# Query projection moved into the first FFN's Strassen units, w2 sums in PSUM, two products on one bank: a new order for a one-core attention and FFN kernel

## The chip, the cores and the metric

The kernel runs on one core of a Trainium2 chip, in one launch. The metric is the device time in microseconds (us). Besides the time of plain runs there is one profiled execution, whose span (first to last instruction) is a little shorter than the time of its run. The engines have the names of the profile: PE (matrix products) with its weight loads PEld, DVE (vector), ACT (activation), POOL (GpSimd) and SP, which issues the DMAs.

## What is computed

`x` is 2048 tokens by 512 features. Layer norm gives xn, and then

```python
q, k, v = xn @ wqkv                                # 32 heads of 16
phi_q = [softmax(q @ w_phi), softmax(-q @ w_phi)]  # per head, 16 wide each
phi_k = [softmax(k @ w_phi), softmax(-k @ w_phi)]
kv = phi_k.T @ v ; z = sum over tokens of phi_k    # per head, not causal
s = (phi_q @ kv) / (phi_q @ z + 1e-6) @ wo
h = xn @ w1 + b1 ; h = h * tanh(softplus(h))       # Mish, 1792 wide
g = silu(h @ w2)
out = x + s * g
```

All of it is in fp32.

## The kernel before, in words

**Products.** Each fp32 product is three fp32r products: an operand is split into a high part (an ACT copy) and a low part (a subtraction on DVE or POOL). The main unit of work on PE is one 128x128 weight tile against 512 columns, "128x512" in the profile. Layer norm (`norm`, L348) works on 16 tiles of 128 tokens; PE transposes each (`pt`), and its high and low parts stay as `xT`. The head map w_phi is folded into the query and key weights on PE (`folded`, L298: `wqf`, `wkf`).

**Keys and values** use a Strassen scheme of seven products for a pair of tiles (`kv_a` to `kv_d`, L470 to L496; banks `kx`, `ky`, `kz`); pair 0 is done plainly. In `kv_a` bank `kx` is copied out (`held`), bank `kz` gets the second product, and DVE adds the two in SBUF (`plus`). `k_soft` makes the two softmaxes of a tile: for tile t, DVE takes maximum and minimum (`kTm<-kp`), subtracts twice (`kTe`), ACT takes the exponential, DVE sums, inverts and scales. `kv_acc` (L518) then adds phi_k transposed times v to the PSUM bank `kvp`, with many small 32x32 matmuls. `sums` (L867) reads `kvp` once all 16 tiles are in.

**Queries** are projected plainly: `q_proj` (L505) makes 12 matmuls of 128x512 for each of the 16 tiles, copies the bank to SBUF (`qs`) and sends it to DRAM (`qd`). `q_soft` (L510) reads it back in another arrangement (`qp`, four DMAs a tile) and does the same softmax. `den` (L534) multiplies by z (`ez`), sums (`tz`), inverts, scales the features, and transposes them into `ph`. `num` (L554) takes four tiles together: 64 small matmuls `pn`. `att_out` (L571) multiplies by wo (`pw`) and sends the result to DRAM (`so`).

**The first FFN product** uses 14 units: two halves q of the tokens by seven blocks b of 256 features, each of seven products (`ffn1a` to `ffn1d`, L689 to L711; banks `fx`, `fy`, `fz`). The x operands are sums of tiles kept in DRAM (`scr`, `scrT`). `load_g` (L650) loads them for one half in 14 DMAs of 512 KB (names `fb..`, `ft..`). `GROUPS` (L33) says which blocks share a load: there are three loads here, L0 to L2. `ffn1a` has the form of `kv_a`: `held`, `fz`, then `plus` on DVE (`ha<-ha,fz`). `prep1` (L586) makes the sums of a block of w1 (`w1a`, `w1s` with h or l).

**The second FFN product** (`ffn2a` to `ffn2f`, from L739; banks `x`, `y`, `z`) uses sums of w2, which `prep2`, `prep2d`, `prep2a` and `prep2b` (L613 to L634) make in SBUF (`w2r`, `w2c`, `w2s`, `w2t`), with the splits (`w2x`, `w2t`, `w2sb`) on DVE or POOL. `final` (L811) puts silu, product and sum together.

**Order.** `ORDER` (L34) is the order in which parts of the program are built. `SCHED` (L49) is the order in which the single operations are issued; a letter behind a number picks the engine (V, G or A) where two could do it. `PLACE` (L134) gives each tile its buffer. The pools are `slot` (38 big buffers), `s2` (15 of 128x512), `rq` (5), `ps` (the 8 PSUM banks) and a few more. Each engine takes its instructions strictly as listed, and `Program.issue` emits all of them, so each has line L192 in the profile (L194 after the change). Groups are therefore told apart by the tiles' names.

Of the kernel before, what the change touches and what calls it, by code (L numbers as in the profile page):

```python
# [10 lines left out]
F32 = mybir.dt.float32  # L11
# [5 lines left out]
P = 128  # L17
# [10 lines left out]
SLOTS, S2, RQ = 38, 15, 5  # L28
# [4 lines left out]
GROUPS = ((0, 1, 2, 3), (4, 5, 6))  # L33
ORDER = """  # L34
wq1 N0 wk0 N4 wk1 N1 K0 wq0 Ka1 Q4 wv0 wv1 V0 N5 N2 ws0 Q0 Q2 N8 Q5 ws1 N12 N3 V4
Q8 Kb1 Q1 N6 Q12 ws2 Ka3 N7 Ka2 Kc1 N9 ws3 Kb2 N10 Q6 Kd1 Kc2 Q9 N13 N11 Kd2 Kb3 Ka5 Ka4
Kc3 Ka7 K4 Kd3 Ka6 N14 Kb4 Kb6 Kc4 Q11 N15 Kc6 Q14 Kd4 Kb5 Q13 A0 P2 A1 Q10 Q3 Kd6 A2 A3
P1 A4 Kc5 Q7 Kb7 Q15 Kd5 L0 Kc7 Fa2 Kd7 P0 Fa1 S1 Fa0 S0 Fb1 Fc1 Fb2 Fb0 Fd1 Fc2 A5 A6
S2 A7 P3 Fa3 Fb3 Fc3 Fc0 Fd2 b1 S3 Fd3 z D0 D1 Fd0 L1 Fa7 S4 Fa8 Fa9 Fa10 D2 Fb7 S6
D3 Fb8 Fc8 Fb9 Fd8 P4 Fc9 Fb10 Fd9 S10 Fa11 Fc10 Fc7 Fd10 D4 P5 P6 S5 Fd7 Fb11 Fc11 Fa13 D5 Fb13  # L40
Fa12 S7 S8 Fc13 Fb12 Fc12 Fd13 D6 L2 S9 Fd11 Fa4 Fb4 D7 S13 Fd12 wo0 Fa5 Fc4 Fa6 Fb6 Fc6 Fb5 Fd6
Fc5 wo1 U0 D8 D9 Fd4 Fd5 U1 R0 D10 O7 Ga0 O4 R1 O0 S11 Ga1 D11 R2 O3 S12 Ga2 O2 R3
D12 Ga3 D13 S14 R4 O6 Ga4 O1 O5 R5 D14 Ga5 S15 D15 R6 U2 Ga6 U3 T0 O13 Gb0 T1 Gb1 T2
Gb2 O11 T3 Gb3 T4 Gb4 T5 O8 Gb5 T6 Gb6 B0 Gc0 O14 B1 Gc1 B2 Gc2 B3 Gc3 O15 B4 Gc4 B5
Gc5 B6 O9 Gc6 C0 Gd0 C1 Gd1 O12 C2 Gd2 C3 Gd3 C4 O10 Gd4 C5 Gd5 C6 Gd6 E0 Ga7 Ga8 Ga9
E1 Ga10 Ga11 Ga12 E4 Ga13 Gb7 E5 Gb8 Gb9 Gb10 E6 Gb11 Gb12 E7 Gb13 Gc7 Gc8 Gc9 Gc10 Gc11 Gc12 Gc13 E8
E2 E3 E9 E14 E15 E12 E13 Ge7 Ge8 Ge9 Ge10 Ge11 Ge12 Ge13 E10 Gf7 Gf8 Gf9 Gf10 Gf11 Gf12 Gf13 E11
"""
# [156 lines left out]
def block_kernel(ctx: ExitStack, tc: tile.TileContext, x, xt, wqkT, wv, phi, wo, w1, b1, w2, out):  # L205
# [200 lines left out]
    def proj(t, w, name):  # L406
        ps = bank([P, D], f"{name}{t}")
        for i in range(0, KC, 2):
            with one():
                for k in (i, i + 1):  # L410
                    mm3(ps, (xT[t][:, 0, k, :], xT[t][:, 1, k, :]), w[k], k == 0, k == KC - 1)
# [511 lines left out]
```

## Time and profile before

| | |
|---|---|
| plain runs | 491.93, 492.81 and 681.34 us, median 492.81 |
| the profiled execution | 491.45 us, its span 489.7 us |
| PE busy | 477.8 us, 98% of the span |
| DVE busy | 448.3 us, 92% |
| ACT busy | 292.5 us, 60% |
| POOL busy | 267.2 us, 55% |
| DMA | 114.01 MB, mean 233 GB/s |

A group's row in the profile names the engine, the operation, out<-in by the program's names, the shapes and the count; behind the bar stand the busy time, the mean of one in ns, and the idle time just before with the releaser. Matmuls overlap, so the mean of one (some 390 ns) is longer than the distance from one to the next. The same holds of DVE: its records overlap by some 0.08 us, and the distance between starts is what one costs. The profiled execution lies 1.75 us over its span, and the median of the runs 3.1 us over it.

### The profile page before, as it was taken

To read this page: it belongs to the slowest core of one execution; us is meant where nothing else is said; L and a number is where in the kernel's file an instruction comes from. 1 tells how busy PE (TensorE), PEld (TensorE's weight loads), DVE (VectorE), ACT (ScalarE), POOL (GpSimd) and SP (SyncE) were. 2 spreads that over 40 slices of the span, in tenths; PEclk is the share of its full clock that TensorE was granted. 3 is DMA by queue.
4 is the path that set the end of the run, shared out by engine and by line. 5 is a ranking of instruction groups with operands and counts; after the bars stand their busy time and mean duration, and the time that the engine had idled before them with its cause. 6 is when DMAs were issued, how large, how long until landed. Compare 5 with 4: busy or idle time off the path is not lost.

```text
span 489.7 us, 9113 instructions
## 1 busy us (share of the span) xinstructions
PE 477.8 (98%) x3332; PEld 386.9 (79%) x3332; DVE 448.3 (92%) x716; ACT 292.5 (60%) x465; POOL 267.2 (55%) x185
## 2 busy tenths in 40 slices
PE   9999899999999999999999999999899999999995
PEld 9888678888787887888888867868678888888883
DVE  5989999999999999999999989999998977799965
ACT  5998675544262351325434558694795879889531
POOL 2678942323427333164825399968867647541540
PEclk9999999999999999999999999999999999999998
DMA  8524447595979777996999999972247747933276
GB/s 297 200 90 149 193 173 242 183 346 199 331 233 308 264 259 251 301 319 198 349 324 314 322 301 346 338 229 87 104 178 251 229 145 230 299 111 87 86 220 231
DMA packets 71133, 114.01 MB, mean 233 GB/s; under 512 B 6193, under 2 KB 39601, under 8 KB 71089
## 3 DMA queue, kind: packets, MB, share of 16 engines
q1 hardware_dynamic: 70944, 113.18, 68.8%
q8 instruction: 26, 0.43, 0.3%
q10 hardware_dynamic: 144, 0.26, 0.2%
q14 instruction: 19, 0.15, 0.1%
HBM read 71.47 MB, written 41.94 MB: 232 GB/s over the span
## 4 chain that ended last, share of the span: by engine, by line
PE 73%; DVE 10%; issue 3%; DMA 1%; ACT 1%; POOL 0%; DVEq 0%; SPq 0%; ACTq 0%
PE fx L192 16%; PE x L192 14%; PE y L192 8%; PE fy L192 7%; PE kx L192 6%; PE fz L192 4%; PE pw L192 4%; PE q L192 4%; PE ky L192 3%; PE z L192 2%; PE kvp L192 2%; PE kz L192 2%; DVE tz L192 1%; PE pn L192 1%; DMA so<-so 1%
## 5 line engine op out<-in xcount | busy, mean ns | idle before, releaser
L192 PE MATMUL q<-wqh,xT 128*128 128x512 f32 x128 | 42.2, 392 | 0.0
L192 ACT ACTIVATE r<-r,b1t 128x512 f32<-128x512 f32 x56 | 37.7, 713 | 0.1
L192 PEld LDWEIGHTS q<-wqh,xT 128*128 128x128 f32 x128 | 24.0, 188 | 5.2
L192 POOL TENSOR_TENSOR w1sl<-w1s,w1sh 128x1024 fp32r<-128x1024 f32 x7 | 16.8, 2406 | 20.1 <-ACT w1sh L192 16.4
L192 POOL TENSOR_TENSOR rs<-rs,mhalf 128x1 f32<-128x1 f32 x16 | 10.0, 641 | 29.4 <-DVE rs L192 25.1
L192 POOL TENSOR_TENSOR tl<-ts,th 128x1024 fp32r<-128x1024 f32 x8 | 19.4, 2431 | 10.4 <-ACT th L192 5.1
L192 PE MATMUL q<-wql,xT 128*128 128x512 f32 x64 | 25.0, 390 | 0.0
L192 DVE TENSOR_REDUCE tz<-ez 128x64 f32<-128x1024 f32 x16 | 19.3, 1208 | 0.3
L192 ACT ACTIVATE ha<-fx 128x512 f32<-128x512 f32 x14 | 8.2, 594 | 17.6 <-PE fx L192 14.0
L192 ACT ACTIVATE hd<-fx 128x512 f32<-128x512 f32 x13 | 7.7, 595 | 17.7 <-PE fx L192 14.4
L192 ACT ACTIVATE hc<-fx 128x512 f32<-128x512 f32 x13 | 7.6, 594 | 17.7 <-PE fx L192 17.7
L192 POOL TENSOR_TENSOR w1al<-w1a,w1ah 128x768 fp32r<-128x768 f32 x6 | 11.1, 1849 | 12.3 <-DMA scr<-xT 6.5
L192 PE MATMUL kx<-wss,th 128*128 128x512 f32 x56 | 17.6, 394 | 0.0
L192 ACT ACT_TABLE_LOAD x13 | 16.7, 1283 | 1.5 <-PEq L915 1.2
L192 ACT ACTIVATE hb<-fx 128x512 f32<-128x512 f32 x13 | 7.7, 595 | 13.8 <-PE fx L192 12.0
L192 ACT ACTIVATE kp<-kx 128x512 f32<-128x512 f32 x12 | 7.2, 596 | 14.7 <-PE kx L192 10.8
L192 POOL TENSOR_TENSOR mt<-r,r 128x512 f32<-128x512 f32 x7 | 9.5, 1364 | 11.6 <-ACT oh L192 4.4
L192 PE MATMUL pw<-oh,wo0l 128*128 128x512 f32 x32 | 12.6, 392 | 2.2 <-DVE h L192 2.2
L192 POOL TENSOR_TENSOR t<-r,mt 128x512 f32<-128x512 f32 x8 | 12.6, 1573 | 3.2 <-DVE mt L192 1.9
L192 PEld LDWEIGHTS q<-wql,xT 128*128 128x128 f32 x64 | 12.0, 188 | 2.5
L192 POOL TENSOR_TENSOR w2t<-w2t 128x512 f32<-128x512 f32 (+1 forms) x10 | 12.8, 1281 | 0.1
L192 PE MATMUL pw<-oh,wo0h 128*128 128x512 f32 x32 | 12.5, 389 | 0.0
(977 smaller groups left out, 1865.0 us busy)
## 6 DMA issues: line engine op xcount, KB each, us to landing
r<-hd SPq DMA_DIRECT2D x28, 512.0 KB, 5.5
qd<-qs SPq DMA_DIRECT2D x16, 256.0 KB, 4.0
scr<-xT SPq DMA_DIRECT2D x8, 512.0 KB, 6.3
scrT<-th SPq DMA_DIRECT2D x8, 512.0 KB, 4.3
scrT<-tl SPq DMA_DIRECT2D x8, 512.0 KB, 5.9
qp<-qd SPq DMA_DIRECT2D x64, 64.0 KB, 5.2
so<-so SPq DMA_DIRECT2D x16, 256.0 KB, 5.3
sr<-so SPq DMA_DIRECT2D x16, 256.0 KB, 3.6
```

The lines of the kernel that those rows point to most:

```text
L192: getattr(g, m)(*a, **k)
```

## The change

- **Queries.** `proj`, `q_proj` and the way through DRAM go. The folded query weights are written as two more blocks in the form of w1 (`w1a7`, `w1a8`); `prepq` makes their sums; four more units (two halves of the tokens, two blocks) run through `ffn1a` to `ffn1d`. Such a unit's results go by a DVE transpose straight into `qp`.
- **Query softmax.** The sums stay as they are, without an inverse; the product of both sums takes its place in `den`. `rq` has 7 buffers of four values a head.
- **Two products on one bank.** In `ffn1a` and `kv_a`, ACT copies the first product into the bank of the second, PE adds the second to it, and the bank is sent or copied. The DVE sum goes.
- **w2 sums** are formed in PSUM banks, from an ACT copy, with DVE operations that have one operand there; their splits are on DVE alone.
- **Loads.** `GROUPS` has four loads (L0 to L3): blocks 0 to 2, then the two query blocks with block 3, then 4 to 6.
- `final` keeps `u` in SBUF for two token tiles, the head order of wo's rows is another, and `ORDER`, `SCHED` and `PLACE` are new lists.

```diff
-SLOTS, S2, RQ = 38, 15, 5
+SLOTS, S2, RQ = 38, 15, 7
-GROUPS = ((0, 1, 2, 3), (4, 5, 6))
+GROUPS = ((0, 1, 2), (NB, NB + 1, 3), (4, 5, 6))
...
+        if sums is not None:
+            V.tensor_reduce(sums, e, axis=X, op=ALU.add)
+            return e
...
     def kv_a(p):
         kv_product(x, t, 0, 0, True)
-        kp[t] = held(x, f"kp{t}")
-        kv_product(z, t, 1, 1, True)
-        plus(kp[t], z)
+        A.activation(z, x, AF.Copy)
+        kv_product(z, t, 1, 1, False)
+        kp[t] = held(z, f"kp{t}")
...
-    def q_proj(t):
-        p = s2(f"qs{t}")
-        copy(p, proj(t, w["q"], "q"))
-        Q.dma_start(qd[t], p)
-
     def q_soft(t):
-        p = s2(f"qp{t}")
-        for c in range(4):
-            Q.dma_start(p[32 * c:32 * c + 32, :].rearrange("p (b f) -> p b f", b=4),
-                        qd[t][:, c * P:(c + 1) * P].rearrange("(b p) f -> p b f", p=32))
-        rq[t] = alloc("rq", [P, 2 * H], f"q{t}r")
-        eq[t], _ = softmax(p, f"q{t}", rq[t])
+        r = rq[t] = alloc("rq", [P, H, 4], f"q{t}r")
+        eq[t] = softmax(qp.pop(t), f"q{t}", r[:, :, 0:2])
+        A.activation(r[:, :, 2], r[:, :, 0], AF.Copy)
+        V.scalar_tensor_tensor(r[:, :, 3], r[:, :, 0], 1e-6, r[:, :, 1], op0=ALU.mult, op1=ALU.mult)
...
+    def in_psum(a, name):
+        ps = bank([P, a.shape[1], 2 * P], name)
+        A.activation(ps, a, AF.Copy)
+        return ps
...
     def prep2a(b):
         a = load_w2(b, "w2s")
-        either(a[:, 3], a[:, 2], a[:, 3], op=ALU.add)
-        either(a[:, 2], a[:, 3], a[:, 0], op=ALU.subtract)
-        pair2(b, 2, a[:, 2:4])
+        ps = bank([P, 2, 2 * P], f"pa{b}")
+        A.activation(ps[:, 1], a[:, 3], AF.Copy)
+        V.tensor_tensor(ps[:, 1], ps[:, 1], a[:, 2], op=ALU.add)
+        V.tensor_tensor(ps[:, 0], ps[:, 1], a[:, 0], op=ALU.subtract)
+        pair2(b, 2, a[:, 2:4], ps)
...
-    def put(n, h, second, j2):
+    def send(n, h, second, j2):
+        if isinstance(n, tuple):
+            q, b = n
+            t = 4 * (2 * q + second) + 2 * (b - NB) + j2
+            qp[t] = s2(f"qp{t}")
+            V.transpose(qp[t], h)
+            return
         q, b = divmod(n, NB)
+        if h.space == "PSUM":
+            h = held(h, f"h{'ad'[j2]}{n}")
...
     def ffn1a(n):
-        x, z = bank([P, D], f"fx{n}"), bank([P, D], f"fz{n}")
+        x, z = bank([P, D], f"fx{tag(n)}"), bank([P, D], f"fz{tag(n)}")
         product(x, n, 0, 0, True)
-        h = held(x, f"ha{n}")
-        product(z, n, 1, 1, True)
-        plus(h, z)
-        put(n, h, 0, 0)
+        A.activation(z, x, AF.Copy)
+        product(z, n, 1, 1, False)
+        send(n, z, 0, 0)
...
+        for j in range(2):
+            ps = folded(wqT, "wq", i, j).rearrange("p (b f n) -> p b f n", b=2, f=2)
+            for b in range(2):
+                copy(qa[b][:, 0:4:3, j * P:(j + 1) * P] if i == 0 else qa[b][:, 1:3, j * P:(j + 1) * P], ps[:, b])
```

**How the lists move the work.** Three places follow, each as the instructions stand on one engine. First the start of PE, up to the first key product `k`. The names are: `wake`, matmuls on ones; `pt`, transposes of x tiles; `wkf` and `wqf`, folded weights. Before, with all eleven `wake` ahead of these rows:

```order
L192 MATMUL wkf_175<-phit,wkT_141 128x128 x4
L192 MATMUL wkf_159<-phit,wkT_139 128x128 x4
L192 MATMUL pt_155<-ident,x_149 128x128 x4
L192 MATMUL wkf_176<-phit,wkT_142 128x128 x4
L192 MATMUL wkf_160<-phit,wkT_140 128x128 x4
L192 MATMUL wqf_147<-phit,wqT_143 128x128 x4
L192 MATMUL wqf_192<-phit,wqT_188 128x128 x4
L192 MATMUL pt_167<-ident,x_161 128x128 x4
L192 MATMUL wqf_193<-phit,wqT_189 128x128 x4
L192 MATMUL wqf_148<-phit,wqT_144 128x128 x4
L192 MATMUL pt_183<-ident,x_177 128x128 x4
L192 MATMUL k_184<-wkh_157,xT_153 128x512
```

Of the change, with six `wake`, a `pt`, a `wkf` and three more `wake` ahead of these rows:

```order
L194 MATMUL pt_145<-ident,x_139 128x128 x4
L194 MATMUL wkf_130<-phit,wkT_123 128x128 x4
L194 MATMUL wake<-ones 128x128
L194 MATMUL wkf_131<-phit,wkT_124 128x128 x4
L194 MATMUL wake<-ones 128x128
L194 MATMUL pt_209<-ident,x_202 128x128 x4
L194 MATMUL wqf_471<-phit,wqT_467 128x128 x4
L194 MATMUL pt_217<-ident,x_210 128x128 x4
L194 MATMUL wqf_475<-phit,wqT_473 128x128 x4
L194 MATMUL wkf_153<-phit,wkT_125 128x128 x4
L194 MATMUL wqf_472<-phit,wqT_468 128x128 x4
L194 MATMUL pt_161<-ident,x_155 128x128 x4
```

The same pieces stand ahead of the first `k`, but the last key weight, `wkf_153`, is now nearly the last of them.

The second place is DVE up to the scaling of tile 3's key features, `k3e`, for which PE's `kvp` matmuls wait. Before, this is row 157 of DVE:

```order
L192 TENSOR_REDUCE k3m<-k3e 128x64
L192 TENSOR_TENSOR kp_322<-kp_322,ky_321 128x512
L192 RECIPROCAL k3m<-k3m 128x64
L192 TENSOR_REDUCE k6m<-kp_322 128x32
L192 COPY v_374<-kx_289 128x512
L192 TENSOR_TENSOR k3e<-k3e,k3m 128x1024
```

Of the change, where it is row 196, with tiles 7, 8, 9 and 12 in work before it:

```order
L194 TENSOR_REDUCE k3m<-k3e 128x64
L194 RECIPROCAL k3m<-k3m 128x64
L194 TENSOR_SCALAR nb_381<-mv_376,rs_379 128x1
L194 COPY v_286<-ones 128x16
L194 COPY v_374<-ones 128x16
L194 TENSOR_TENSOR k7e<-k7e,k7m 128x1024
L194 TENSOR_REDUCE k12m<-kp_322 128x32
L194 TENSOR_SCALAR nb_362<-mv_357,rs_360 128x1
L194 TENSOR_SCALAR rs_419<-mv_416 128x1
L194 TENSOR_TENSOR k3e<-k3e,k3m 128x1024
```

And on PE where these features are used, of the change:

```order
L194 MATMUL fz_348<-fb1h_329,w1al_293 128x512
L194 MATMUL fz_348<-fb1l_330,w1ah_292 128x512
L194 MATMUL fz_348<-fb1h_329,w1ah_292 128x512
L194 MATMUL kvp<-v_289,k3e 32x32 x16
L194 MATMUL pt_363<-ident,x_356 128x128 x4
L194 MATMUL kvp<-v_286,k7e 32x32 x16
L194 MATMUL kvp<-v_289,k3e 32x32 x16
```

Before, this `kvp` stands at PE's row 318, now at row 275. Ahead of it stand 312 matmuls of 128x512 now and 366 before.

The third place is DVE ahead of the second group of query tiles (4 to 7) that `num` takes; `ph_714` is its operand. Of the change:

```order
L194 RECIPROCAL tz_773<-tz_773 128x32
L194 TENSOR_TENSOR tz_773<-q6r,tz_773 128x64
L194 TENSOR_TENSOR q6e<-q6e,tz_773 128x1024
L194 TENSOR_TENSOR q7e<-q7e,tz_778 128x1024
L194 STREAM_TRANSPOSE ph_714<-q7e 128x1024
L194 TENSOR_TENSOR pb_950<-pb_950,w2t_949 128x512
L194 STREAM_TRANSPOSE ph_714<-q6e 128x1024
```

The last row is DVE's row 560. On PE 1218 matmuls of 128x512 stand ahead of the `pn` that use it. The two groups of tiles 8 to 15 are taken earlier in the list than these, and all four groups are done before the second FFN product begins. Before, the last groups of `pn` and `pw` stand among the second FFN product's matmuls.

More of the change, by code (lines that the diff above doesn't have):

```diff
@@ L326, in block_kernel @@
     scrT = [dram.tile([P, 4, 2, 4, 2, P], F32, name=f"scrT{q}") for q in range(2)]
-    qd = [dram.tile([P, D], F32, name=f"qd{t}") for t in range(NT)]
     xT, tT, pts = {}, {}, {}
@@ L404, in kv_product, with softmax @@
                     PE.matmul(ps, u[:, k], v[:, k], start=first and k == 0 and i == 0, stop=k == 1 and i == 2, skip_group_check=True)
[L406 to L411, printed above, removed]
-        return ps
-    def softmax(p, name, r=None):
+    def softmax(p, name, sums=None):
         p3 = p.rearrange("p (h d) -> p h d", d=DH)
@@ L558, in num @@
             for a in range(2):
-                for m in range(4):
-                    for c in range(4):
-                        at = slice(32 * c, 32 * c + 32)
-                        PE.matmul(pn[c][32 * m:32 * m + 32, :], w["kvw"][at, m, a, :], ph[at, :, 2 * m + a, :],
+                for c in range(4):
+                    for j in range(4):
+                        at = slice(32 * j, 32 * j + 32)
+                        PE.matmul(pn[j][32 * c:32 * c + 32, :], w["kvw"][at, c, a, :], ph[at, c, :, a, :],
                                   start=a == 0, stop=a == 1, skip_group_check=True)
@@ L609, in pair2 @@
             t = slot([P, 2, m, 2 * P], f"w2x{b}_{n}", F32R)
-        split(src, t[:, 0], t[:, 1], either)
+        split(ps, t[:, 0], t[:, 1])
         w2_[b, n] = t
+    def in_psum(a, name):
+        ps = bank([P, a.shape[1], 2 * P], name)
+        A.activation(ps, a, AF.Copy)
+        return ps
     def prep2(b):
@@ L629, in prep2a @@
         a = load_w2(b, "w2s")
-        either(a[:, 3], a[:, 2], a[:, 3], op=ALU.add)
-        either(a[:, 2], a[:, 3], a[:, 0], op=ALU.subtract)
-        pair2(b, 2, a[:, 2:4])
+        ps = bank([P, 2, 2 * P], f"pa{b}")
[3 more added lines that the diff above has]
+        pair2(b, 2, a[:, 2:4], ps)
     def prep2b(b):
         a = load_w2(b, "w2t")
-        either(a[:, 0:2], a[:, 0:2], a[:, 2:4], op=ALU.subtract)
-        either(a[:, 1], a[:, 1], a[:, 0], op=ALU.add)
-        pair2(b, 3, a[:, 0:2])
+        ps = in_psum(a[:, 0:2], f"pb{b}")
+        V.tensor_tensor(ps, ps, a[:, 2:4], op=ALU.subtract)
+        A.activation(a[:, 0], ps[:, 0], AF.Copy)
+        V.tensor_tensor(ps[:, 1], ps[:, 1], a[:, 0], op=ALU.add)
+        pair2(b, 3, a[:, 0:2], ps)
     hd, part, t4, hd2 = {}, {}, {}, {}
@@ L662, in product @@
     def product(ps, n, a, x, first):
-        q, b = divmod(n, NB)
+        q, b = n if isinstance(n, tuple) else divmod(n, NB)
         ah, al = w1_[b][0:2] if a < 3 else w1_[b][2:4]
@@ L687, in plus, with tag, unit @@
         V.tensor_tensor(t, t, ps, op=ALU.add)
+    def tag(n):
+        return "q%d" % (2 * n[0] + n[1] - NB) if isinstance(n, tuple) else str(n)
+    def unit(f):
+        return lambda i: f((i // 2, NB + i % 2))
     def ffn1a(n):
-        x, z = bank([P, D], f"fx{n}"), bank([P, D], f"fz{n}")
+        x, z = bank([P, D], f"fx{tag(n)}"), bank([P, D], f"fz{tag(n)}")
         product(x, n, 0, 0, True)
-        h = held(x, f"ha{n}")
-        product(z, n, 1, 1, True)
-        plus(h, z)
-        put(n, h, 0, 0)
+        A.activation(z, x, AF.Copy)
+        product(z, n, 1, 1, False)
+        send(n, z, 0, 0)
         part[n] = [x]
     def ffn1b(n):
-        x, y = part[n][0], bank([P, D], f"fy{n}")
+        x, y = part[n][0], bank([P, D], f"fy{tag(n)}")
         product(x, n, 4, 4, False)
-        part[n] += [y, held(x, f"hb{n}")]
+        part[n] += [y, held(x, f"hb{tag(n)}")]
         product(y, n, 3, 3, True)
@@ L706, in ffn1c @@
         product(x, n, 5, 5, False)
-        h = held(x, f"hc{n}")
+        h = held(x, f"hc{tag(n)}")
         plus(h, y)
-        put(n, h, 1, 1)
+        send(n, h, 1, 1)
     def ffn1d(n):
@@ L713, in ffn1d @@
         product(x, n, 2, 6, False)
-        put(n, held(x, f"hd{n}"), 0, 1)
+        send(n, x, 0, 1)
         product(y, n, 6, 2, False)
         plus(h, y)
-        put(n, h, 1, 0)
+        send(n, h, 1, 0)
     ym, xb, yb, zb, hs = {}, {}, {}, {}, {}
@@ L817, in final @@
         Q.dma_start(st, sdram[n])
-        u = h if h.space == "PSUM" else bank([P, D], f"u{n}")
+        u = s2(f"u{n}") if n in PIECES else h if h.space == "PSUM" else bank([P, D], f"u{n}")
         k = D // PIECES.get(n, 1)
@@ L825, in final @@
             Q.dma_start(out[at[0], g * D + i:g * D + i + k], xx[:, c])
-    w = {n: [None] * KC for n in "qo"}
+    w = {"o": [None] * KC}
     w["kv"], w["k"], w["v"] = [None] * 7, [None] * 2, [None] * 2
@@ L858, in weights_q @@
         wqT[2 * i:2 * i + 2] = load_wT(0, "wq", i, 2)
-        w["q"][2 * i:2 * i + 2] = fold(wqT, "wq", i)
+        if i == 0:
+            for b in range(2):
+                qa[b] = slot([P, 4, 2 * P], f"w1a{NB + b}")
+        for j in range(2):
+            ps = folded(wqT, "wq", i, j).rearrange("p (b f n) -> p b f n", b=2, f=2)
+            for b in range(2):
+                copy(qa[b][:, 0:4:3, j * P:(j + 1) * P] if i == 0 else qa[b][:, 1:3, j * P:(j + 1) * P], ps[:, b])
     def weights_o(i):
@@ L881, in block_kernel @@
              "wk": weights_k, "wv": weights_v, "ws": weights_s, "wq": weights_q, "wo": weights_o, "N": norm,
-             "Ka": kv_a, "Kb": kv_b, "Kc": kv_c, "Kd": kv_d, "K": k_plain, "V": v_plain, "A": kv_acc, "Q": q_proj, "S": q_soft, "D": den, "U": num,
+             "Ka": kv_a, "Kb": kv_b, "Kc": kv_c, "Kd": kv_d, "K": k_plain, "V": v_plain, "A": kv_acc, "Pq": prepq, "Qa": unit(ffn1a), "Qb": unit(ffn1b), "Qc": unit(ffn1c), "Qd": unit(ffn1d), "S": q_soft, "D": den, "U": num,
              "O": att_out, "L": load_g, "P": prep1, "R": prep2, "T": prep2a, "B": prep2b, "C": prep2d,
@@ L909 @@
         "phi": np.ascontiguousarray(phi),
-        "wo": np.ascontiguousarray(A_wo),
+        "wo": np.ascontiguousarray(np.asarray(A_wo).reshape(4, 4, 32, D).transpose(1, 0, 2, 3).reshape(D, D)),
         "w1": np.ascontiguousarray(np.stack(w1b, 2).reshape(NB, P, 4, 2 * P)),
```

234 lines of the change are left out of this document (119 added, 115 removed), and 41 rows, old and new, of the table PLACE.

## The prediction

> **What bounds the kernel now.** I read the engines' busy time first, then PE's clock and the chain of waits, then the windows.
>
> ```profile
> span 489.7 us, 9113 instructions
> PE 477.8 (98%) x3332; PEld 386.9 (79%) x3332; DVE 448.3 (92%) x716; ACT 292.5 (60%) x465; POOL 267.2 (55%) x185
> PEclk9999999999999999999999999999999999999998
> PE 73%; DVE 10%; issue 3%; DMA 1%; ACT 1%; POOL 0%; DVEq 0%; SPq 0%; ACTq 0%
> ```
>
> PE is the bound at full clock, DVE is close behind, and the chain lies on PE for 73% of the span and on DVE for 10%. The windows show where PE has gaps (columns: stretch, length, busy PE, PEld, DVE, ACT, POOL, clock, DMA share, GB/s).
>
> ```profile
> 0.00:20.00 20.00, 18.88 (x125) 17.84 (x126) 14.61 (x39) 13.53 (x29) 6.33 (x15) 1.00 0.83 304
> 20.00:94.00 74.00, 72.57 (x553) 58.92 (x556) 68.46 (x145) 53.86 (x102) 47.78 (x36) 1.00 0.44 155
> 94.00:154.00 60.00, 59.43 (x809) 48.09 (x809) 56.53 (x86) 28.86 (x47) 22.59 (x19) 1.00 0.82 276
> 154.00:284.00 130.00, 129.88 (x819) 105.48 (x826) 126.99 (x207) 50.74 (x77) 60.51 (x37) 1.00 0.88 294
> 284.00:347.00 63.00, 60.30 (x395) 46.04 (x388) 60.80 (x91) 46.12 (x69) 55.38 (x35) 1.00 0.72 248
> 347.00:484.00 137.00, 136.78 (x652) 110.57 (x651) 119.33 (x149) 98.82 (x143) 74.59 (x47) 1.00 0.58 184
> ```
>
> PE idles in the first 94 us and from 284 to 347; elsewhere it is full. DVE idles 5.39, 5.54, 3.47, 3.01 and 2.20 us in the first five stretches. That is 5.4 at the start and 14.2 later, up to 347 us.
>
> Now I need what PE could do at best. From the chain (start, length):
>
> ```profile
> 91.21 1.39 PE kx L192 x6
> 213.31 1.36 PE fy L192 x6
> 345.98 0.69 DVE h L192
> 346.71 8.46 PE pw L192 x36
> 474.94 8.85 PE x L192 x39
> ```
>
> Six matmuls of 128x512 take 1.36 us, 0.2268 each. I put prices on PE's whole list in its order: 0.2268 for these; 0.39 for a `wake`, 0.224 for a folded weight, 0.13 for a transpose, 0.028 for a `kvp` and 0.076 for a `pn`, from the distances of their records. That gives pure PE work up to any place. Before, it is 88.3 us at the `kx` that starts at 91.21, so 2.9 us are lost by then. It is 336.3 at the `pw` that starts at 346.71: 10.4 lost. From there on nothing more is lost, up to the last matmul at 483.79 (work 474.9, lost 8.9, which differs by the coarse prices). So the losses lie at the start and in the stretch that ends at `pw`, where the chain comes out of DVE's `h`.
>
> The same for DVE, in distances between starts:
>
> ```profile
> 107.07 0.69 DVE L192 TENSOR_TENSOR k12e<-kp,k12m 128x512 f32<-128x512 f32 x1
> 107.67 0.68 DVE L192 TENSOR_TENSOR k12e<-k12m,kp 128x512 f32<-128x512 f32 x1
> 108.28 1.21 DVE L192 TENSOR_TENSOR k7e<-k7e,k7m 128x1024 f32<-128x1024 f32 x1
> 109.48 1.23 DVE L192 TENSOR_REDUCE k12m<-k12e 128x64 f32<-128x1024 f32 x1
> 110.75 0.57 DVE L192 RECIPROCAL k12m<-k12m 128x64 f32<-128x64 f32 x1
> 111.22 1.17 DVE L192 TENSOR_REDUCE k8m<-k8e 128x64 f32<-128x1024 f32 x1
> 118.97 0.41 DVE L192 TENSOR_TENSOR ts<-pt,ts 128x256 f32<-128x256 f32 x1
> 119.30 0.41 DVE L192 TENSOR_TENSOR w1s<-w1s,w1a 128x256 f32<-128x256 f32 x1
> ```
>
> A 128x512 costs 0.60 (0.61 as a reduction), a 128x1024 1.20 (1.15 when reduced or transposed), an inverse 0.49, a 128x256 0.30, one value a token 0.13, up to 64 values 0.16. Their sum, compared with where DVE really is, gives its dead time: idle time and slowed operations together. At the second of these rows, the copy into `so`,
>
> ```profile
> 283.30 1.17 DVE L192 TENSOR_REDUCE tz<-ez 128x64 f32<-128x1024 f32 x1
> ...
> 347.04 0.63 DVE L192 COPY so<-pw 128x512 f32<-128x512 f32 x1
> ```
>
> the sum is 318.4, so 28.6 us are dead (at the first it is 262.5): 5.4 at the start, 14.2 of later idle time, and some 9 of slowed operations. One kind of these:
>
> ```profile
> L192 DVE TENSOR_TENSOR w2x<-w2r,w2x 128x512 fp32r<-128x512 f32 x4 | 5.1, 1296 | 0.0
> L192 DVE TENSOR_TENSOR h<-h,y 128x512 f32<-128x512 f32 x4 | 2.7, 682 | 0.1
> ```
>
> With both operands in SBUF while POOL works, a 128x512 takes 1296 ns; with one in PSUM it takes 682. The Trainium skill, page "SBUF — State Buffer", section "Who interferes with whom", states that a DVE instruction with two SBUF inputs contends with a GpSimd instruction that reads SBUF, and that one with at most one does not; these two rows agree.
>
> **The change, part by part.**
>
> *PE work.*
>
> ```profile
> L192 PE MATMUL q<-wqh,xT 128*128 128x512 f32 x128 | 42.2, 392 | 0.0
> L192 PE MATMUL q<-wql,xT 128*128 128x512 f32 x64 | 25.0, 390 | 0.0
> ```
>
> These 192 matmuls go. Four units of seven products of six matmuls come, 168. 24 fewer at 0.2268 make **-5.4 us**; all else on PE keeps its count. The Trainium skill, "Perfetto Trace Analysis", section "Identifying the Most-Contended Engine", calls matmul busy time a bad measure of distance to roofline and takes that of LDWEIGHTS instead; by the 188 ns of a load here it would be 24 x 0.188 = 4.5 us. I keep the distance of records, since the six in 1.36 us show what the list moves by.
>
> *DVE work.*
>
> ```profile
> L192 DVE TENSOR_TENSOR ha<-ha,fz 128x512 f32<-128x512 f32 x14 | 9.4, 679 | 0.5 <-PE fz L192 0.5
> L192 DVE TENSOR_TENSOR kp<-kp,kz 128x512 f32<-128x512 f32 x7 | 4.8, 680 | 0.2 <-ACT kp L192 0.2
> ```
>
> The 21 sums go (12.6 us at 0.60), and 16 inverses of the query softmax (7.8). There come 16 transposes into `qp` (9.6 at 0.60), eight sums of query units (4.8), 32 short operations that replace 16 (some 2.6), and the w2 sums and splits that POOL did. Over the whole list it is 418 before and 429 after, 11 more, in 469 us of PE work. Which is late is then a matter of the place.
>
> *The start.* The Q products were cheap for DVE and filled PE while DVE did norms. They now stand behind load L1, and FFN units and key tiles come early. At tile 3's `k3e`, DVE's list holds before: 53 x 0.60, 13 x 0.61, 6 x 1.20, 5 x 1.15, 15 x 0.30, 5 x 0.49, 49 x 0.13 and 11 of 3.6 in all, together 69.6, and PE had 108.0 ahead of the `kvp` that needs it. Of the change: 62 x 0.60, 21 x 0.61, 10 x 1.20, 9 x 1.15, 20 x 0.30, 9 x 0.49, 56 x 0.13 and the same 3.6, together 93.7, and PE has 93.7 ahead. DVE's slack of 38 us is gone, so all its dead time up to there is lost on PE.
>
> ```profile
> 3.78 0.69 DVE L192 BATCH_NORM_STATS2 st<-x 128x6 f32<-128x512 f32 x1 [2.71 <-DMA x<-x]
> 13.82 0.48 PE L192 MATMUL k<-wkh,xT 128*128 128x512 f32 x1
> ```
>
> DVE can't begin before x lands at 3.8 us, so 3.5 are lost at least. With the whole 5.4 of the first window and 1 more it is 6.5, against 2.9 before. It should show at the first `k` already, which now needs the split of the last key weight, behind 14.0 to 15.3 us of DVE work: 18 to 20 us, where it was 13.82. Behind a waiting `kvp` the whole PE list waits.
>
> *The query softmax.* The next tight place is the second group of `num` (tiles 4 to 7): DVE has 310.8 us of work ahead of the last `ph_714`, PE 317.4 ahead of its `pn`. What PE has lost by then is DVE's dead time less 6.5. Bounds: with 5.4 at the start, no later idle time, and 3 of slowed operations (most of the slowed ones were w2's, which now read PSUM), 8.4 are dead and 1.9 lost, though the start costs more, so 5.4 is the least; with the 28.3 that were dead before `pw`, 21.8. I take 5.4, half the later idle time (7.1, since DVE waits less for a PE that isn't ahead of it), and 5 of slowed operations, 17.5 dead: **11.0 lost**, start included.
>
> *PSUM banks.* The w2 sums add 28 tenants to the eight banks.
>
> ```profile
> L192 PE MATMUL pw<-oh,wo0l 128*128 128x512 f32 x32 | 12.6, 392 | 2.2 <-DVE h L192 2.2
> ```
>
> One wait for a bank, 2.2 us, is there now. An added one costs 0 to 2.2; I take 1.0. So 12.0 are lost against 10.4: **+1.6**.
>
> *Two products on one bank* adds an ACT copy, a 594 ns record, between `fx` and `fz`. PE has 18 other matmuls (4.1 us) between them in the unit ahead of `k3e`. Hidden; bare, 18 units and 7 pairs would cost 25 x 0.6 = 15. ACT is busy 60%, and PE leaves it 4 us.
>
> *DMA.*
>
> ```profile
> qd<-qs SPq DMA_DIRECT2D x16, 256.0 KB, 4.0
> qp<-qd SPq DMA_DIRECT2D x64, 64.0 KB, 5.2
> ```
>
> 16 x 256 KB and 64 x 64 KB go, 8.4 MB and 80 issues of SP. The fourth load adds 14 x 512 KB, 7.3 MB, at the 294 GB/s of 154 to 284 us 25 us of transfer. It is issued with a unit's products between it and its use, and the traffic it adds is less than what goes. Nothing; uncovered, a few us.
>
> *After `pn`* the second FFN product's 133 us of PE work have some 100 of DVE work beside them. Nothing lost there, as before, and the last 5.9 us behind the last matmul stay.
>
> Sum: -5.4 + 1.6 = -3.8. Span 489.7 - 3.8 = 485.9; its run 1.75 over that, 487.65; and as the median lay 1.36 over the profiled run, **489.0 us** on the scale of the medians.
>
> **Rivals.**
>
> *A: DVE's later idle time vanishes.* The lists then lose only the 6.5 of the start. For it: all w2 contention goes, and POOL's list shrinks. Against: DVE idled in every stretch. -5.4 - 3.9 = -9.3, 483.5 us.
>
> *B: slower, DVE starves PE.* DVE's dead time at tiles 4 to 7 stays what it was before `pw`, 28.3, with PE 6.5 ahead: 21.8 lost, 11.4 more than before, +6.0 in all, 498.8 us. It decides once 15.8 are lost (10.4 + 5.4), that is from 22.3 dead. For it: DVE is 92% busy, and from 284 to 347 us it did 55.9 us of work in 63.7. Against: part of this idle time came from a PE that ran late itself.
>
> *C: the banks.* ACT's copy, PE's second product and a w2 sum each hold a bank; if four of them end in a 2.2 us wait, +8.8 - 1.0 makes 496.8. The Trainium skill, "Perfetto Trace Analysis", section "Optimization Strategy", says that consistent bubbles can mean that SBUF or PSUM ran out; no run shows it yet. I count C with B.
>
> **How the numbers follow.** Forecast (486 to 492.8): 0.50. A (under 486): 0.20. B and C (over 492.8): 0.30. The losses of 5.4 and 24.0 (21.8 + 2.2) bound it at 482.4 and 501.0; leaving a tenth out at either end, the range is 483 to 499. About 2% is what a measurement can tell from no change: below 482.95 lies the far end of A, 0.07; above 502.67 the far end of B, 0.05; 0.88 lie between.
>
> **What would show it.** Right: the first `k` at 18 to 20 us; 5 to 8 us lost by the `kvp` of `k3e`; some 11 by the `pn` of `ph_714`; no gap behind it; w2 splits near 680 ns. Wrong: `fz` waiting for ACT, PE waiting for DMA `fb` or `ft`, PE gaps behind 350 us, or a dead time of DVE over 22 us at `ph_714`.

## The result: 5.8 us faster, and the profile after

The changed kernel takes 486.9 us (median of four runs, 486.45 to 488.28) against 492.81 before (median of three runs; a fourth, of 681.34 us, was in a slow state and is left out). The ratio of the means, 487.13 and 492.89 us, is 0.9883 (0.9847 to 0.9919): 5.8 us faster with an interval of 4.0 to 7.5. Forecast were 489.0 and a sum of -3.8. The profiled execution has a span of 484.7 us where it was 489.7; each is the fastest execution of its kernel in this comparison. Below, a difference from the changed kernel is the difference of two ratios to the kernel before, times 493 us.

The page of the changed kernel first, its busy times and the chain that ended last:

```profile
PE 473.3 (98%) x3308; PEld 383.3 (79%) x3308; DVE 444.7 (92%) x748; ACT 315.5 (65%) x535; POOL 250.4 (52%) x168
PEclk8999999999999999999999999999999999999998
PE 94%; DVE 2%; issue 1%; DMA 1%; ACT 0%; POOL 0%; ACTq 0%
```

The chain lies on PE for 94% now (73% before), and DVE's share fell from 10 to 2%. PE's busy time fell by 4.5 us, DVE's by 3.6. The windows (columns as in the prediction) show that the gaps sit elsewhere:

```profile
0.00:20.00 20.00, 15.00 (x101) 14.39 (x102) 13.13 (x52) 15.19 (x38) 9.06 (x22) 0.91 0.89 317
20.00:94.00 74.00, 73.81 (x702) 60.09 (x701) 71.71 (x135) 60.33 (x110) 63.16 (x43) 1.00 0.71 243
94.00:154.00 60.00, 58.96 (x690) 47.85 (x688) 54.40 (x88) 28.61 (x48) 13.94 (x11) 1.00 0.78 264
154.00:284.00 130.00, 129.89 (x753) 106.17 (x752) 128.20 (x219) 64.63 (x104) 63.39 (x39) 1.00 0.70 229
284.00:330.00 46.00, 46.00 (x416) 32.49 (x415) 44.83 (x81) 33.98 (x62) 14.96 (x9) 1.00 0.87 310
330.00:347.00 17.00, 17.00 (x77) 14.06 (x76) 16.12 (x27) 14.31 (x28) 15.31 (x9) 1.00 0.71 224
347.00:479.00 132.00, 132.00 (x578) 108.06 (x577) 114.56 (x148) 97.83 (x152) 70.61 (x39) 1.00 0.56 183
```

PE idles 5.0 us in the first 20 (1.1 before), and not at all where it lost 2.7 before, from 284 to 347. The long waits of PE, by the view of waits:

```profile
PE pt L194 <- DVE st L194: 3.9, 1, 3.9
PE wake L194 <- DVE mhalf L276: 1.1, 1, 1.1
PE fx L194 <- issue: 1.0, 1, 1.0
PE kvp L194 <- issue: 0.2, 1, 0.2
```

One wait carries most of it, the first transpose, and this is how it and the places that the prediction named look in the timeline:

```profile
7.93 1.09 PE L194 MATMUL pt<-ident,x 128*128 128x128 f32 x4 [3.89 <-DVE st L194]
19.20 0.50 PE L194 MATMUL k<-wkh,xT 128*128 128x512 f32 x1
99.09 1.21 DVE L194 TENSOR_TENSOR k3e<-k3e,k3m 128x1024 f32<-128x1024 f32 x1
100.52 0.46 PE L194 MATMUL kvp<-v,k3e 128*32 128x32 f32 x32
312.77 2.35 PE L194 MATMUL pn<-ph,kz 32*32 32x512 f32 x64
324.58 1.23 DVE L194 STREAM_TRANSPOSE ph<-q6e 128x1024 f32<-128x1024 f32 x1
326.18 2.35 PE L194 MATMUL pn<-ph,kz 32*32 32x512 f32 x64
469.98 9.68 PE L194 MATMUL x<-me,w2x 128*128 128x512 f32 x42
```

With the prediction's prices, PE's pure work is 2.3 us ahead of that first `pt`, 13.1 ahead of the first `k`, 93.6 ahead of the `kvp` of `k3e`, 304.0 and 317.3 ahead of the two `pn`, and 469.4 in all. So PE has lost 5.6, 6.1, 6.9, 8.8 and 8.9 us at these places, and 10.3 at the last matmul, which ends at 479.66. DVE's `k3e` ends 0.2 us before PE uses it, its last `ph` 0.4 us before the `pn`: the two engines arrive together, and PE waits for DVE at neither place.

Before, in the timeline:

```profile
341.60 0.39 PE L192 MATMUL pw<-oh,wo0l 128*128 128x512 f32 x1
346.71 0.50 PE L192 MATMUL pw<-oh,wo0l 128*128 128x512 f32 x1 [2.23 <-DVE h L192]
474.77 9.00 PE L192 MATMUL x<-me,w2x 128*128 128x512 f32 x39
```

The `pw` that starts at 346.71 is the second tile of its group, not the first; 339.1 us of pure work stand ahead of it, and 7.6 us were lost there, not 10.4 as the prediction has it. At the last matmul (483.77) it was 8.9.

The account of the 5.0 us of span: -5.4 of PE work, +1.4 lost by PE (10.3 against 8.9), -0.9 behind the last matmul (484.7 - 479.66 = 5.0, against 5.9). By places, PE loses 5.3 more up to the first `k` (6.1 against 0.8) and 3.9 less from there to the end (4.2 against 8.1).

### The profile page after: what moved, and what is told of

It reads as the page before. It is cut to its first block, busy times and chain, and to the rows that moved or that the text cites. A ratio compares the mean times of both kernels' runs of the same rounds, so it can differ in the third digit from the quotient of the medians.

```text
span 484.7 us, 9045 instructions
## 1 busy us (share of the span) xinstructions
PE 473.3 (98%) x3308; PEld 383.3 (79%) x3308; DVE 444.7 (92%) x748; ACT 315.5 (65%) x535; POOL 250.4 (52%) x168
## 2 busy tenths in 40 slices
DMA packets 67004, 112.96 MB, mean 233 GB/s; under 512 B 5136, under 2 KB 37520, under 8 KB 66960
## 4 chain that ended last, share of the span: by engine, by line
PE 94%; DVE 2%; issue 1%; DMA 1%; ACT 0%; POOL 0%; ACTq 0%
PE fx L194 15%; PE x L194 15%; PE pw L194 9%; PE kx L194 8%; PE y L194 8%; PE fy L194 7%; PE ky L194 4%; PE fz L194 4%; PE fxq L194 4%; PE z L194 4%; PE kvp L194 2%; PE kz L194 2%; PE fyq L194 2%; PE pn L194 2%; PE pt L194 2%
## 5 line engine op out<-in xcount | busy, mean ns | idle before, releaser
L194 POOL TENSOR_TENSOR w1al<-w1a,w1ah 128x768 fp32r<-128x768 f32 x9 | 16.7, 1855 | 30.3 <-DVE q11e L194 24.0
L194 POOL TENSOR_TENSOR mt<-r,r 128x512 f32<-128x512 f32 x9 | 15.4, 1719 | 31.7 <-ACT oh L194 18.6
L194 POOL TENSOR_TENSOR w1s<-w1a 128x256 f32<-128x256 f32 x16 | 11.8, 745 | 9.7 <-PE fy L194 6.9
L194 ACT ACTIVATE fz<-fx 128x512 f32<-128x512 f32 x14 | 8.0, 580 | 13.4 <-DVE v L194 8.1
L194 ACT ACTIVATE u<-h 128x512 f32<-128x512 f32 x12 | 7.0, 597 | 14.1 <-DVE h L194 14.1
L194 POOL TENSOR_TENSOR md<-t,md 128x512 fp32r<-128x512 f32 x5 | 9.8, 1971 | 10.8 <-ACT md L194 10.8
L194 ACT ACTIVATE ha<-fz 128x512 f32<-128x512 f32 x13 | 7.7, 594 | 11.5 <-PE fz L194 7.1
L194 DVE TENSOR_TENSOR u<-u,sr 128x512 f32<-128x512 f32 (+2 forms) x18 | 10.1, 571 | 4.0 <-ACT u L194 3.9
L194 PE MATMUL pt<-ident,x 128*128 128x128 f32 x64 | 9.9, 287 | 3.9 <-DVE st L194 3.9
L194 POOL TENSOR_TENSOR mt<-r,mt 128x512 f32<-128x512 f32 x9 | 12.9, 1436 | 0.3
```

What stands on the lines that cost most here:

```text
L194: getattr(g, m)(*a, **k)
```

## The experiments

My theory behind the sum: in the new list PE and DVE run level, so the work of each counts. The rivals: PE bounds alone, or DVE does. Eleven kernels test this.

**One engine at a time, in the changed kernel.** `q28less` and `q28more` take away or add PE work in the query units:

```diff
                 for i, (u, v) in enumerate(((al, xh), (ah, xl), (ah, xh))):
+                    if isinstance(n, tuple) and k == 1 and i == 1:
+                        continue
                     PE.matmul(ps, ...
```

> The changed kernel with one of the six matmuls left out in each of the 28 products of the query units (low-order terms of the queries are missing from the output): 28 x 0.2268 = 6.35 us less for PE, nothing less for the others. Theory: DVE is the next bound; its last transposes before the groups of tiles 0 to 3 and 4 to 7 end 0.3 and 0.4 us before PE uses them, so PE waits there for what it saved: 0.3 to 2 us faster. Rival (PE alone bounds): 6.4 us faster.

Measured: ratio 0.9911 (0.9886 to 0.9936), 1.4 us above the changed kernel, which the two intervals don't separate from nothing. 6.35 us less on PE gave nothing. Of the traces I compare one stretch, from the `kvp` of `k3e` to the first `pn` of tiles 0 to 3, since executions differ by up to 3 us ahead of it. In the changed kernel it is 312.77 - 100.52 = 212.25 us; here

```profile
103.46 0.46 PE L194 MATMUL kvp<-v,k3e 128*32 128x32 f32 x32
315.89 2.35 PE L194 MATMUL pn<-ph,kz 32*32 32x512 f32 x64
```

212.43. And the view of waits shows in what small pieces PE gave the time back:

```profile
PE fx L194 <- ACT fz L194: 1.5, 1, 1.5
PE fx L194 <- issue: 1.4, 1, 1.4
...
PE fx L194 <- DVE hc L194: 0.8, 1, 0.8
PE fzq L194 <- ACT fzq L194: 0.8, 1, 0.8
PE fx L194 <- POOL w1sl L194: 0.6, 1, 0.6
PE fz L194 <- ACT fz L194: 0.4, 1, 0.4
```

It waits for ACT's copies between the first two products, for DVE and for POOL, none of which stood in the changed kernel's list of waits. These rows sum to 5.5 us, where the changed kernel has 1.0 in the stretch. So PE doesn't bound alone, as the theory has it, but the place is another: no `pn` waits for DVE's last transposes, and the largest share, 2.7 us, is for ACT's copies. Behind the longest of those, 1.5 us, stands DVE again, since ACT itself came late to that copy:

```profile
220.95 0.58 ACT L194 ACTIVATE fz<-fx 128x512 f32<-128x512 f32 x1 [2.67 <-DVE q12e L194]
```

`q28more` does that matmul twice instead.

> The changed kernel with one of the six matmuls done twice in each of the 28 products of the query units (a low-order term is counted twice in the output): 28 more on PE. Theory: each costs its distance of 0.2268 us, 6.4 us slower. By the 188 ns of a weight load it would be 5.3 us. Rival: PE has waits behind them that take some of it up, under 3 us slower.

Measured: 0.9992 (0.9974 to 1.001), 5.4 us slower than the changed kernel. The stretch is 318.56 - 100.84 = 217.72, 5.5 longer. The time alone doesn't tell this from the 5.3 that the weight loads would make. The distances do: the 196 query matmuls start 0.2274 us apart on the mean here, the 168 of the changed kernel 0.2295. So 28 matmuls cost 6.35, and by that price PE lost 1.9 us in the stretch in the changed kernel (8.8 - 6.9) and 1.0 here. The difference of 0.9 came out of small delays between matmuls, not out of the waits that the list shows (1.0 us at `fx` in the changed kernel, 1.4 here).

`sums21` gives DVE back the 21 sums that the change took from it:

```diff
+            if i in self.more:
+                t, z = self.more[i]
+                self.eng["V"].tensor_tensor(t, t, z, op=ALU.add)
...
         kp[t] = held(z, f"kp{t}")
+        prog.more[len(prog.ops) - 1] = kp[t], z
```

> The changed kernel with the 21 DVE sums of 128x512 that the change removed put behind the copies again (each adds the second bank once more, which the output shows); PE, ACT and the banks do as before. Theory: DVE is as critical as PE; seven of them stand ahead of k3e, 4.2 us, which is lost there at once, and all 21, 12.6 us, ahead of tiles 0 to 3's features; DVE's idle time between the two places takes up to 5 of it, so 7 to 12 us slower. Rival: DVE is off the path, under 2 us slower.

Measured: 1.0321 (1.0296 to 1.0346), 21.6 us slower than the changed kernel. The direction is the theory's, the size far above it: the stretch grew by 15.5 us (334.25 - 106.50 = 227.75), more than the 12.6 of all the sums, and 6.0 more were lost ahead of it. In this list a sum stands right behind ACT's copy, and DVE waits for that too (5.7 us at `ha` in its view of waits), and all behind it waits along. Two more things are in the 21.6. The added sum reads the second product's bank once more, so the banks do not do as before: PE, which reads no result of these sums, waits 6.1 us for two `ha`. And after waits of 2.0 and 4.0 us PE's granted clock was 0.50, from 268.6 to 272.0 and from 295.9 to 299.3 us, with matmuls of 128x512 0.43 us apart instead of 0.23, some 3 us more. So the run shows that the sums are dear in this place, and not the price of 12.6 us of DVE work.

`dve36less` takes other DVE work away, `less_both` that and the 28 matmuls:

```diff
         h = held(x, f"hc{tag(n)}")
-        plus(h, y)
+        prog.ops.append({})
         send(n, h, 1, 1)
```

> The changed kernel with the 36 DVE sums of the third and the last products left out in the 14 units of the first FFN and the four of the queries (terms are missing from the output): 21.6 us less for DVE, the same for PE. Theory: PE and DVE run level, so that one alone can give no more than what PE lost between the first k and the second group of tiles 0 to 7, 8.9 - 6.3: 0.5 to 2.6 us faster. Rival: DVE is the bound by itself, 10 us faster or more.

> The changed kernel with both left out, the 28 query matmuls (6.35 us of PE) and the 36 DVE sums (21.6 us of DVE). Theory: PE could not use its 6.35 us because DVE ran level with it; with DVE lightened it can: 6 to 9 us faster. Rival: something else (ACT's copies, banks, loads) held PE in the run q28less: under 3 us faster.

Measured: 0.9871 (0.9842 to 0.9899) for `dve36less`, 0.6 us under the changed kernel, not told apart from nothing; its stretch is 211.10, 1.15 less. 0.9788 (0.9758 to 0.9818) for `less_both`, 4.7 us under it. So PE alone gave nothing, DVE alone next to nothing, and both together 4.7: level, as the theory says. But 6 to 9 were expected, and 4.7 lies between the theory and its rival. The stretch is

```profile
102.64 0.46 PE L196 MATMUL kvp<-v,k3e 128*32 128x32 f32 x32
310.85 2.35 PE L196 MATMUL pn<-ph,kz 32*32 32x512 f32 x64
```

208.21, 4.0 less, and PE still loses 4.2 in it: 1.4 at `fx` with nothing shown, 0.9 for POOL's `w1sl`, 0.4 for ACT. With PE and DVE lighter, POOL and ACT show next.

**w2 sums.** `w2sbuf` puts 20 of 28 preparations back in SBUF:

```diff
+    def in_sbuf(a):
+        next(places)
+        prog.ops.append({})
+        return a
...
-        pair2(b, 0, a, in_psum(a, f"pr{b}"))
+        pair2(b, 0, a, in_sbuf(a) if b in (0, 1, 2, 3, 4, 5, 6) else in_psum(a, f"pr{b}"))
```

> The changed kernel with 20 of its 28 preparations of w2 sums back in SBUF (still on DVE, without ACT's copy into a bank; all seven of w2r, three of w2c, four of w2s, six of w2t). Theory: DVE's records with both operands in SBUF are slowed while POOL works, w2x<-w2r from some 680 to 1000 to 1300 ns, but most of them stand behind the last num, where PE does not wait for DVE: within 1 us of the changed kernel (486.9). Rival: the sums ahead of the second group of num push it, 2 to 4 us slower.

Measured: 1.0197 (1.0172 to 1.0222), 15.5 us slower than the changed kernel. The theory was wrong on the size. Three groups of it in the changed kernel, and the same work in `w2sbuf`:

```profile
L194 DVE TENSOR_TENSOR w2x<-pr,w2x 128x512 fp32r<-128x512 f32 x7 | 4.8, 679 | 0.1
L194 DVE TENSOR_TENSOR w2x<-pa,w2x 128x512 fp32r<-128x512 f32 x7 | 4.8, 682 | 0.7 <-ACT w2x L194 0.7
L194 DVE TENSOR_TENSOR w2x<-pc,w2x 128x256 fp32r<-128x256 f32 x7 | 2.9, 419 | 3.2 <-ACT w2x L194 3.2
```

```profile
L196 DVE TENSOR_TENSOR w2x<-w2r,w2x 128x512 fp32r<-128x512 f32 x7 | 9.9, 1409 | 0.0
L196 DVE TENSOR_TENSOR w2x<-w2s,w2x 128x512 fp32r<-128x512 f32 x4 | 6.2, 1544 | 2.2 <-ACT w2x L196 2.2
L196 DVE TENSOR_TENSOR w2x<-w2c,w2x 128x256 fp32r<-128x256 f32 x3 | 4.9, 1624 | 2.1 <-ACT w2x L196 2.1
```

One operand in SBUF instead of PSUM costs 0.73, 0.86 and 1.2 us an instruction: with the two SBUF operands of `w2s` itself (941 ns instead of 421) and the others some 19 us. It is POOL's work beside them that does it. Here are two of the `w2x<-w2r` in `w2sbuf`, one beside POOL's `ma2l` and one while POOL stands idle (from 356.1 to 360.6 us), and one `w2x<-pr` of the changed kernel beside POOL's `ma4l` (345.23 to 347.65):

```profile
336.31 2.39 POOL L196 TENSOR_TENSOR ma2l<-r,ma2h 128x1024 fp32r<-128x1024 f32 x1 [1.28 <-DMA w2s<-w]
336.43 2.81 DVE L196 TENSOR_TENSOR w2x<-w2r,w2x 128x512 fp32r<-128x512 f32 x1
359.88 0.67 DVE L196 TENSOR_TENSOR w2x<-w2r,w2x 128x512 fp32r<-128x512 f32 x1
345.73 0.68 DVE L194 TENSOR_TENSOR w2x<-pr,w2x 128x512 fp32r<-128x512 f32 x1
```

That the Trainium skill ("SBUF — State Buffer", "Who interferes with whom") names as an exclusive lock between DVE with two SBUF inputs and a GpSimd instruction that reads SBUF; the rows agree. The stretch up to tiles 0 to 3 is as in the changed kernel (212.63), and the loss comes behind it, where PE had no wait (its busy time from 347 to 479 us is 122.62, where it was 132.00):

```profile
PE x L196 <- DVE so L196: 4.3, 1, 4.3
...
PE x L196 <- DVE w2x L196: 2.9, 1, 2.9
```

PE's waits behind `pn` are 9.8 us in its list. With the two longest its granted clock fell to 0.50, from 351.4 to 354.8 and from 371.9 to 378.7 us, with the matmuls 0.43 us apart instead of 0.23, some 4 us more. So I was wrong that PE doesn't wait for DVE there, and in this run the waits cost more than their length. Not tried is the same with POOL doing part of it, as before the change.

**The parts, in the kernel before.** `before24less` leaves out 24 query matmuls, `before_nosum` the 21 sums, `before_both` both:

```diff
         PE.matmul(ps, al, bh, start=first, stop=False)
-        PE.matmul(ps, ah, bl, start=False, stop=False)
+        if not less:
+            PE.matmul(ps, ah, bl, start=False, stop=False)
...
-        plus(kp[t], z)
+        prog.ops.append({})
```

> The kernel before with 24 of the 192 query matmuls left out (low-order terms of twelve tiles' queries are missing from the output): the saving in PE work alone, 24 x 0.2268 = 5.4 us. Theory: PE is not the only bound; at the last group of pw it waits for DVE, which gets no less to do, so part of it goes into that wait: 1 to 4 us faster. Rival (PE alone bounds): 5.4 us faster.

> The kernel before with the 21 DVE sums of a second product left out (the second product is missing from the output): 12.6 us less for DVE, nothing less for PE. Theory: of the 7.9 us that PE has lost by the last group of pw, those behind the first key products come from DVE, so 2 to 5 us faster. Rival: DVE's work is covered by PE's, under 1 us faster.

> The kernel before with both left out, 24 query matmuls and 21 DVE sums. Theory: PE and DVE each bound part of the way, so both together give at least the sum of the two apart, 8 to 11 us faster; this is what the change could bring without its new start. Rival (PE alone): 5.4 us faster, as with the 24 matmuls left out.

Measured: 0.9929 (0.9900 to 0.9957), 3.5 us faster than before; 0.9976 (0.9958 to 0.9993), 1.2 faster; 0.9919 (0.9892 to 0.9946), 4.0 faster. The first fits. The other two fall short, and `before_both` refutes what I expected of it: in the list before, DVE's 12.6 us were nearly covered. A part of the reason is in the `pw`, here of `before_both`, where the row of before is the one shown above:

```profile
343.44 0.50 PE L194 MATMUL pw<-oh,wo0l 128*128 128x512 f32 x1 [2.22 <-DVE h L194]
```

All of it moves 3.3 us forward (in `before_nosum` it stays, at 346.75), and the wait in front of it stays as it was, 2.2 us in all four kernels. It isn't DVE being late from long before: DVE's timeline shows no wait of its own from 318 to 347 us in `before`, `before_nosum` and `before_both`, and the sum `h` that `pw` waits for stands behind two reductions of 1.2 us each. So I take it that the order of that stretch makes the wait on the spot; no run moves only these instructions. None of the cuts removes it; the change, whose list has all `num` and `pw` ahead of the second FFN product, has no such wait.

**The start.** `start` moves one DVE instruction; `start_warm` has ten more `wake` too.

```diff
-155 156 157 159 0 1
+155 156 0 1
...
-25 26 27 28 29 30 31V 32 366
+25 26 27 28 157 159 29 30 31V 32 366
...
-    for _ in range(WAKE):
-        PE.matmul(wake, ones, ones, start=True, stop=True)
+    for i in range(WAKE):
+        with one():
+            for _ in range(3 if i < 4 else 2 if i < 6 else 1):
+                PE.matmul(wake, ones, ones, start=True, stop=True)
```

> The changed kernel with one DVE instruction (the scaling of tile 2's mean, which waits for ACT) moved behind the statistics of tile 0. Theory: DVE's first 4.22 us of waiting end when ACT's mean is ready (5.29) and not when tile 0's x is there (about 4.5); PE's first transpose, now at 7.93, comes 0.7 to 1.4 us earlier, and since DVE and PE are within 0.5 us of each other at k3e and at both groups of tiles 0 to 7, all that follows moves too: 0.6 to 1.4 us faster in all. Rival: tile 0's x lands no earlier than that, or another engine holds the start: no change, within 0.3 us.

> The changed kernel with tile 0's statistics first on DVE, as in the run start, and 16 matmuls on ones instead of 6 ahead of the first transpose, so that PE has no gap from 4.1 to 7.1 us. Theory: PE's matmuls from 8 to 13 us run at twice the distance (0.23 us for a folded weight instead of 0.11) because of that gap; without it the first k comes at 17 to 18 us instead of 19.2, and the whole is 0.8 to 2 us faster than the changed kernel (486.9). Rival: up to k3e it is DVE and ACT that set the pace, whose work begins no earlier than in the run start: k comes earlier, the kvp of k3e does not, no change within 0.7 us.

Measured: 0.9881 (0.9858 to 0.9905) and 0.9900 (0.9871 to 0.9929); the changed kernel has 0.9883. No change: both rivals hold. The first `pt` did come earlier, at 7.06 in `start`, where the first `k` came later all the same, at 19.58. In `start_warm`

```profile
1.12 6.22 PE L194 MATMUL wake<-ones 128*128 128x128 f32 x32 [1.12 <-DVE mhalf L276]
7.18 0.63 PE L194 MATMUL pt<-ident,x 128*128 128x128 f32 x4
8.06 1.16 PE L194 MATMUL wkf<-phit,wkT 128*128 128x128 f32 x8 [0.25 <-DVE mv L194]
18.45 0.49 PE L194 MATMUL k<-wkh,xT 128*128 128x512 f32 x1
102.05 0.46 PE L194 MATMUL kvp<-v,k3e 128*32 128x32 f32 x32
```

the first `k` comes 0.75 us earlier, and the `kvp` of `k3e` doesn't (100.52 in the changed kernel, 102.80 in `start`). What sets the pace between is not settled: in `start` the chain runs over ACT from 19.5 to 38.5 us, then DVE's `tl`. So these two edits get none of the 5.6 us at the start.

## Why the prediction held, point by point

- **PE work, -5.4.** By count right: the pure work fell from 474.9 to 469.4. Cut from the kernel before, as many matmuls brought 3.5; in the changed kernel, a further cut brings nothing, while 28 matmuls more take back nearly all that the change brought (0.9992).
- **The start.** 6.5 us were forecast lost at `k3e`, 6.9 are; the first `k` was forecast at 18 to 20 us and comes at 19.20. The sums of both lists, 93.7 us each, made this step. One thing was otherwise: most of the loss, 5.6, is one gap in front of the first `pt`, and from there to `k3e` PE has only one wait in its list, of 0.2.
- **The query softmax.** 11.0 forecast lost at the second group of tiles 0 to 7, 8.9 are. The step "half the later idle time and 5 of slowed operations" was too big: DVE's last `ph` ends at 325.81 with 310.8 us of work, 15.0 dead, not 17.5.
- **Banks.** 1.0 was taken, and no wait for a bank is in the list of waits (the 1.0 at `fx` has no cause shown). So rival C did not come.
- **Terms taken as nothing.** PE's list has no wait for ACT's copy and none for a load, and 112.96 MB were moved where it was 114.01. The copy is hidden only just: `q28less` has waits for it at once.
- **The loss before** was misread by 2.8 us at `pw` (7.6, not 10.4), and both kernels lose some 1.3 us in the second FFN product, where I put none. The forecast of 12.0 against 10.4 became 10.3 against 8.9: the levels were off, and the +1.6 of what PE loses more measures +1.4. That these agree is luck in part: the loss up to the last `pn` was put 3.1 too high (12.0 for 8.9), the loss before 2.8 too high, and the two errors cancel.
- **The tail** was taken as unchanged and is 0.9 shorter. It isn't chance: it is 5.07 to 5.09 us long in all nine traces of the changed list and 5.92 to 5.94 in all four of the list before. `final` writes `u` to another place and its operations alternate; no run separates this. So -3.8 became -5.0 in the span. The 5.8 of the runs has an interval that reaches down to 4.0, and the forecast's own 3.8 lies just outside it.
- **w2 sums.** The splits came out at 679 and 682 ns as forecast ("near 680"). What that is worth was sized at some microseconds of slowed operations; in this list it is 15.5 us, waits and a slower PE behind them included.
- **Rival A** (no later idle time of DVE, 483.5) was too fast: PE lost 2.0 more from `k3e` to the second group (8.9 against 6.9), and 21.6 us less on DVE, in `dve36less`, take only 1.15 off the stretch. **Rival B** needed 22.3 us dead, and 15.0 were. How near it was, `sums21` and `w2sbuf` suggest: either of the two other parts taken back, in this list, costs 3.7 and 2.7 times what the whole change brings, though in `sums21` a bank is held longer too.

## What to carry to other kernels

Add up each engine's work along its own order, and compare the sums where one hands over to the other: where the sums are equal, expect each dead microsecond to be lost, and a cut on one engine alone to bring little. Test that with cuts on each engine and on both; here 6.35 us of PE and 21.6 us of DVE gave nothing apart and 4.7 us together. A wait that keeps its length when the work ahead of it is cut is likely to be made by the order on the spot; here it was gone with another order.

## What the runs showed of the hardware

PE starts at half its pace. From the timeline of the changed kernel:

```profile
1.12 2.93 PE L194 MATMUL wake<-ones 128*128 128x128 f32 x12 [1.12 <-DVE mhalf L276]
8.81 1.91 PE L194 MATMUL wkf<-phit,wkT 128*128 128x128 f32 x8
...
12.12 1.06 PE L194 MATMUL wkf<-phit,wkT 128*128 128x128 f32 x8
```

Eight folded-weight records take 1.91 us and, 3.3 us later, 1.06. In `start_warm`, those at 8.06 take 1.16. The theory of `start_warm` gives the gap ahead of the first `pt`, 3.9 us here, as the reason; it is only a part of it. The `wake` records ahead of the gap already start 0.21 us apart, as do those before the change up to 4.87 us, where the distance falls to 0.11, and those of `start_warm` up to 6.17. So it took 3.75 and 5.05 us of matmuls to reach the full pace, and six `wake`, 2.9 us, end before it. In the changed kernel the granted clock was 1.00 only from 4.3 us, when the `wake` were over, and fell to 0.50 in the gap, from 7.7 to 11.1. The Trainium skill ("TensorE: Matmul & The Clock Gate", Part 1) has the clock at half after an idle window of about 3.4 us, which agrees; in `sums21` a wait of 2.0 us came before such a fall. The granted clock of the profile does not always tell it: 0.61 from 8 to 12 us in the changed kernel, 1.00 in `start`, where the distances are 0.21 us up to 13.2. The gap of `start` is 3.0 us long, and there PE had not been at full pace before it.

The same instructions can meet in another way from one execution to the next. PE's wait for DVE's `tl`, which ends at 42 to 43 us, is 1.5 us in five of the traces of the changed list (`start`, `q28less`, `sums21`, `dve36less`, `less_both`) and absent in four. `q28less` differs from the changed kernel only in the query units, behind 145 us, and yet only it has the wait. Without it the `kvp` of `k3e` starts at 100.5 to 102.1 us; with it, `sums21` aside, at 102.6 to 103.5.
